# First chunk's attention: the products of probabilities and v of two heads, issued in alternation

## The chip, the cores and the metric

The kernel runs on one core of a Trainium2 chip. The metric is the device time of one execution in microseconds. Engines are named as in the profile: PE (TensorE; its weight loads are PEld), DVE (VectorE), ACT (ScalarE), POOL (GpSimd), SP (SyncE, which issues all DMAs).

## The reference

Attention with a decay for 4 batches of 8 heads (576 positions, head size 64), then a mixture of 4 experts over the 2304 tokens:

```python
scores = scale * np.matmul(q, k.transpose(0, 1, 3, 2))
log_f = np.log(np.clip(f, 0.0001, 1.0)); cum = np.cumsum(log_f, axis=-1)
scores = np.where(causal, -1e9, scores + cum[:, :, :, None] - cum[:, :, None, :])
attn = softmax(scores)                    # with 1e-09 added to the sum
x = np.matmul(attn, v)                    # as (2304, 512)
for e in range(4):                        # p = domain_probs, normalised
    out += p[:, e:e+1] * (np.maximum(x @ w1[e], 0) @ w2[e])
```

## The kernel before

Tokens are worked in nine chunks of 256. Chunk 0 is the first 256 positions of batch 0. The experts' products can only begin once the attention of chunk 0 is there, and from then on the attention of the other chunks runs between the experts' matmuls. So the program has a **startup**, the function `startup`, which does the attention of chunk 0 for 8 heads (4 pairs of heads, `Job`s with hh = 0 or 1), and a long rest.

The startup's instructions stand on each engine in the order in which they are written (`tc.manual_schedule()`). The rest, up to the last experts, is put in order by the tile framework's scheduler, which simulates the program as it is built: what changes in the startup moves it too.

A head of chunk 0 takes these steps, in fp32, each on the tiles that the profile names:

- scores: `qk_pe` (L760) writes two query tiles, 128x128 and 128x256, to PSUM (tile `s`). A matmul of the program in plain fp32 is two PE instructions of the profile (two passes).
- `qk_min` (L795, DVE) masks them, writes `p` and the row's bound `nm`; `qk_exp` (L810, ACT) takes the exponentials, 128 and 256 columns wide.
- `tr_pe` (L922, PE) turns `p` in three 128x128 transposes into PSUM tile `t`; `tr_copy` moves it to SBUF as `pt`, for hh = 0 on ACT (L930), for hh = 1 on DVE (L932).
- `av_pe` (L938, PE): two products with v, 256 and 128 columns (key tiles jt = 0 and 1), with 64 weight columns. The head hh = 0 writes partitions 0 to 63 of tile `o`, the head hh = 1 partitions 64 to 127 of the same tile: each head uses one half of the array's columns.
- once for a pair: `recip` (L830, L838 on DVE, L841 on POOL) and `spread` (L861, PE, tile `b`) for the sums, and `fin` (L977 on ACT, L978 on DVE), which scales `o` into `x`.

`startup` runs ten steps s. In a step, PE gets the scores of head s+1, then the spread of a finished pair (odd s from 3 on), the transposes of head s, and then the products of head s-1. In the second and third step four small filler matmuls on `mask` (`fill`, L251) stand ahead of the products. The products of head s-1 come one step after its transposes, so that the copy of `t` runs meanwhile. In the last pair the products of both heads follow each other.

The experts' matmuls of the rest are L1140, L1152 and L1195; the attention of later chunks has scores at L760 and products with v at L964 (`av_pair`, f16), where the matmuls of the two heads of a pair already alternate. Their probabilities reach them through DMA transposes (tile `pt`, L913).

Of the kernel before, what the change touches and what calls it, by code (L numbers as in the profile page):

```python
# [8 lines left out]
F32 = mybir.dt.float32  # L9
# [10 lines left out]
CH = 256  # L20
# [158 lines left out]
def fused(ctx: ExitStack, tc: tile.TileContext, qk, v, f, probs, w, out):  # L179
    nc = tc.nc  # L180
# [24 lines left out]
    ps_a = PS("ps_a", 4)  # L205
# [41 lines left out]
    def fill(ps, n):  # L247

        t = mask.bitcast(F16)
        for _ in range(n):  # L250
            nc.tensor.matmul(  # L251
                out=ps[:, 384:], lhsT=t[:, :128], rhs=t[:, :128], start=True, stop=True
            )
# [54 lines left out]
    def decay_parts():  # L308
        nc.scalar.activation(out=nc2[0], in_=ncum, func=AF.Copy)
        nc.vector.tensor_tensor(  # L310
            out=nc2[1], in0=ncum, in1=nc2[0].bitcast(F32), op=ALU.subtract
        )
        for n in range(2):
            nc.sync.dma_start(out=ncd[:, n], in_=nc2[n].bitcast(F32))

    def next_loads():
        for hh in range(2):
            jobs[NPR].load(hh)
            jobs[NPR].far(hh)
        v_load(1)  # L320
# [73 lines left out]
    def x_bound(b):  # L394

        def use(u, r):
            nc.vector.tensor_scalar(
                out=xun[:, b : b + 1], in0=u, scalar1=2.0**-2, scalar2=None, op0=ALU.mult
            )
            nc.vector.tensor_scalar(  # L400
                out=vsc[:, b : b + 1], in0=r, scalar1=2.0**14, scalar2=None, op0=ALU.mult
            )
            known.add(("x", b))

        def top():
            nc.vector.tensor_reduce(
                out=xsc[:, b : b + 1],
                in_=firsts[b].rearrange("p r t h d -> p (r t h d)"),
                op=ALU.max,
                axis=AX.X,  # L410
                apply_absolute_value=True,
            )

        across, exponent, finish = power(1, xsc[:, b : b + 1], f"x{b}", use)
        return top, across, exponent, finish
# [211 lines left out]
    class Job:  # L627
# [303 lines left out]
            else:  # L931
                nc.vector.tensor_copy(out=self.pt[hh], in_=self.tp[hh][:, :384])  # L932

        def av_pe(self, hh):
            if hh == 0:
                self.op[0] = ps_a.tile([128, 512], F32, tag="a", name=f"o{self.nm}")
            for jt in range(2):
                nc.tensor.matmul(  # L938
                    out=self.op[0][64 * hh : 64 * hh + 64, 128 * jt : CH],
                    lhsT=self.vr[:, jt, hh, :],  # L940
                    rhs=self.pt[hh][:, CH * jt : CH * jt + CH - 128 * jt],
                    start=(jt == 0),
                    stop=(jt == 1),
                )

        def av_pair(self):

# [124 lines left out]
    def w_load(n):  # L1072
        if n < 4 * WIDE and n not in wraw:
            if n >= 4 * WIDE - 2:
                wraw[n] = acc_p.tile([128, 1024], F32, tag="acc", name=f"wa{n}")
            elif n % 4 < 2:
                wraw[n] = w_p.tile([128, 1024], F32, tag="w", name=f"w{n}")
            else:
                wraw[n] = wr_p.tile([128, 1024], F32, tag=("wr", "wk")[n % 2], name=f"wr{n}", bufs=4)
            with tc.issue_after(gate[-1].ins) if len(gate) > 5 else nullcontext():  # L1080
                gate.append(nc.sync.dma_start(out=wraw[n], in_=w[unit(n)]))
        elif n in RAWS and n not in wraw:
            i = RAWS.index(n)
            wraw[n] = wr_p.tile([128, 1024], F32, tag=("wr", "wk")[i % 2], name=f"wr{n}", bufs=4)
            nc.sync.dma_start(out=wraw[n], in_=w[unit(n)])
# [853 lines left out]
    def startup():  # L1939

        J = lambda h: heads[h] if 0 <= h < FIRST else (None, None)
        decays()
        bound = x_bound(0)
        for h in range(2):
            heads[h][0].begin(h)
        heads[0][0].qk_pe(0, (0, 1))
        for t in range(2):
            heads[0][0].qk_min(0, t)
        for s in range(FIRST + 2):
            (m, mm), (j, hh), (i, ii), (k, kk) = J(s + 1), J(s), J(s - 1), J(s - 2)  # L1950
            if s == 2:
                bound[3]()
            if i:
                i.tr_copy(ii)
                if ii:
                    i.recip()
            if m:
                if s > 0:
                    m.begin(mm)
                m.qk_pe(mm, m.its)  # L1960
                for t in m.its:
                    m.qk_min(mm, t)
            if s == 1:
                bound[1]()
            if j:
                for t in j.its:
                    j.qk_exp(hh, t)
            if k and kk:
                k.spread()
            if j:  # L1970
                j.tr_pe(hh)
            if i:
                if s < 3:
                    fill(i.tp[ii], 4)
                i.av_pe(ii)
            if k and kk:
                k.fin()
            if s == 0:
                bound[0]()
            if s == 1:  # L1980
                bound[2]()
            for n in {0: (0, 1, 2, 3), 2: (4,), 3: (5,)}.get(s, ()):
                w_load(n)
            if s == 0:
                decay_parts()
            if s == 1:
                nc.sync.dma_start(out=pr_r, in_=probs)
            if s == 2:
                next_loads()
# [4 lines left out]
    with tc.manual_schedule():  # L1994
        startup()
# [161 lines left out]
```

## Time and profile before

| | us |
|---|---|
| median of 3 runs | 872.95 |
| runs | 872.12 to 874.1 |
| profiled execution | 873.64 |
| its span, first to last instruction | 871.8 |

The profiled execution is 0.69 above the median. Its span is 1.84 shorter than its own time. In a row of the timeline, the first two numbers are the start and the length in microseconds; consecutive instructions of one kind are merged (xcount), and a bracket gives the idle time of the engine before them and what ended it.

### The profile page before, as it was taken

How to read it: one execution, taken by the hardware profiler on the slowest of the kernel's cores; microseconds unless marked ns; L12 is line 12 of the kernel's file. 1: busy time of each engine (PE TensorE's matmuls, PEld its weight loads, DVE VectorE, ACT ScalarE, POOL GpSimd, SP SyncE). 2: the span in 40 equal slices, each digit the busy share in tenths (PEclk: the TensorE clock that was granted, in tenths of full speed). 3: DMA queues.
4: the chain of work that ended last, by engine and by line, in shares of the span. 5: the costliest groups of instructions: out<-in, count | busy, mean ns of one | idle time of the engine just before them, and what ended most of it. 6: DMA issues, size and time to landing. Idle time of an engine off the chain costs nothing.

```text
span 871.8 us, 16423 instructions
## 1 busy us (share of the span) xinstructions
PE 858.9 (99%) x5843; PEld 570.9 (65%) x5843; DVE 675.9 (78%) x1464; ACT 494.6 (57%) x1021; POOL 392.6 (45%) x439
## 2 busy tenths in 40 slices
PE   9999999999999999999999999999999999999998
PEld 5766666666666676766666666644466666666677
DVE  5866789868777888776768865546798988998897
ACT  5463645756555765656568653436655565655640
POOL 4253423543232422333332304907974898677530
PEclk9999999999999999999999999999999999999999
DMA  8999598799999899968979953433422343431103
GB/s 272 391 220 369 135 290 222 200 345 243 251 235 227 264 275 283 263 161 202 268 215 290 283 102 60 137 129 107 136 98 73 97 145 99 144 121 49 50 2 97
DMA packets 167679, 164.61 MB, mean 189 GB/s; under 512 B 104918, under 2 KB 129548, under 8 KB 167596
## 3 DMA queue, kind: packets, MB, share of 16 engines
q1 hardware_dynamic: 167596, 163.56, 67.4%
q8 instruction: 46, 0.75, 0.3%
q14 instruction: 37, 0.30, 0.1%
HBM read 117.75 MB, written 21.64 MB: 160 GB/s over the span
## 4 chain that ended last, share of the span: by engine, by line
PE 67%; DVE 12%; POOL 8%; DMA 5%; ACT 4%; issue 3%; SPq 1%; ACTq 0%; POOLq 0%; DVEq 0%
PE l L1195 18%; PE l L1152 15%; PE y L1527 10%; PE m L1527 8%; PE s L760 4%; PE o L964 3%; PE l L1140 3%; POOL wt L1344 3%; DMA raw<-in_qk 3%; DVE acc L1223 2%; PE s L783 2%; POOL bs L1416 2%; DVE w L1108 2%; DMA pt<-z 1%; DVE h L1590 1%
## 5 line engine op out<-in xcount | busy, mean ns | idle before, releaser
L1152 PE MATMUL l<-y,w 128*128 128x256 f16 x1728 | 211.5, 273 | 0.0
L1152 PEld LDWEIGHTS <-w 128*128 128x128 f16 x1728 | 163.8, 98 | 40.2 <-issue 7.6
L1195 PE MATMUL l<-w,gh 128*128 128x512 f16 (+1 forms) x600 | 184.4, 392 | 2.3 <-DVE acc L1223 1.7
L694 POOL CAST q<-raw 64x320 fp32r<-64x320 f32 (+1 forms) x56 | 25.2, 451 | 223.3 <-PE s L783 102.0
L1195 PE MATMUL l<-w,gl 128*128 128x512 f16 x284 | 107.2, 379 | 0.8 <-DVE gl L1169 0.8
L810 ACT ACTIVATE p<-p,nm 128x384 f32<-128x384 f32 (+3 forms) x96 | 62.0, 646 | 64.7 <-DVE nm L795 64.5
L1223 DVE SCALAR_TENSOR_TENSOR acc<-y,scg,acc 128x256 f32<-128x256 f32 (+1 forms) x204 | 93.8, 484 | 4.7 <-PE y L1527 4.6
L1527 PE MATMUL m<-rh,bs 128*128 128x512 f16 x256 | 86.4, 379 | 1.1 <-ACT r L1614 1.1
L1195 PEld LDWEIGHTS <-gh 128*128 128x128 f16 x568 | 51.1, 98 | 51.3 <-issue 10.7
L701 POOL TENSOR_TENSOR kl<-raw,hi 64x576 fp32r<-64x576 f32 (+1 forms) x56 | 66.5, 1188 | 38.7 <-ACT hi L692 35.1
L1527 PEld LDWEIGHTS <-h 128*128 128x128 f16 x672 | 65.7, 98 | 18.0 <-issue 0.6
L795 DVE CUSTOM_DVE_ANT_0 p<-s,mask 128x384 f32<-128x384 f32 (+3 forms) x96 | 54.3, 573 | 28.3 <-PE s L760 25.5
L898 DVE SCALAR_TENSOR_TENSOR z<-p,rs,z 128x512 f16<-128x512 f32 x96 | 61.0, 678 | 18.9 <-ACT z L897 18.9
L692 ACT ACTIVATE hi<-raw 128x896 fp32r<-128x896 f32 (+1 forms) x56 | 45.0, 807 | 37.9 <-DMA raw<-in_qk 16.5
L897 ACT ACTIVATE z<-p,rs 128x512 f16<-128x512 f32 x96 | 52.9, 613 | 22.5 <-issue 8.0
L1527 PE MATMUL m<-rh,bw 128*128 128x512 f16 x191 | 64.4, 379 | 0.1
L1169 DVE SCALAR_TENSOR_TENSOR gl<-l,gh 128x512 f16<-128x512 f32 x72 | 49.2, 683 | 17.5 <-ACT gh L1164 16.9
L1527 PEld LDWEIGHTS <-bs 128*128 128x128 f16 x384 | 37.5, 98 | 37.2 <-issue 1.6
L1527 PE MATMUL y<-bt,h 128*128 128x256 f16 x504 | 61.1, 273 | 0.3 <-DVE acc L1223 0.3
L1590 DVE SCALAR_TENSOR_TENSOR h<-s,h 128x512 f16<-128x512 f32 x56 | 58.2, 1050 | 2.0 <-ACT h L1584 1.7
L1416 POOL TENSOR_TENSOR bs<-wt,bs 128x512 f16<-128x512 f32 x32 | 42.5, 1338 | 35.9 <-ACT bs L1410 35.9
L1164 ACT ACTIVATE gh<-l 128x512 f16<-128x512 f32 (+1 forms) x80 | 46.9, 586 | 20.6 <-PE l L1152 17.8
(386 smaller groups left out, 1763.2 us busy)
## 6 DMA issues: line engine op xcount, KB each, us to landing
wr<-in_w SPq DMA_DIRECT2D x68, 512.0 KB
wd<-w SPq DMA_DIRECT2D x32, 512.0 KB
w<-wd SPq DMA_DIRECT2D x32, 512.0 KB
raw<-in_qk SPq DMA_DIRECT2D x32, 448.0 KB
wp<-in_w SPq DMA_DIRECT2D x36, 256.0 KB
bv<-wd SPq DMA_DIRECT2D x32, 256.0 KB
bw<-wd SPq DMA_DIRECT2D x32, 256.0 KB
raw<-in_qk SPq DMA_DIRECT2D x24, 256.0 KB
```

The costliest lines, as they stand in the source:

```text
L701: nc.gpsimd.tensor_tensor(out=kl[:64, :wk], in0=r[:64, ko : ko + wk], in1=hi[:64, ko : ko + wk].bitcast(F32), op=ALU.subtract,)
L795: nc.vector.tensor_tensor_reduce(out=pt[:, a:z], in0=ps, in1=mask2 if t == 4 and n else mask[:, m0 + a : m0 + z], scale=-0.125, scalar=BIG ...
L810: nc.scalar.activation(out=pt[:, :w_], in_=pt[:, :w_], func=AF.Exp, scale=-1.0, bias=self.nmax[hh][:, c : c + 1], accum_out=self.ssum[:, h ...
L897: nc.scalar.activation(out=o[:, 0], in_=x, func=AF.Copy, scale=sc)
L898: nc.vector.scalar_tensor_tensor(out=o[:, 1], in0=x, scalar=sc, in1=o[:, 0], op0=ALU.mult, op1=ALU.subtract)
L1152: nc.tensor.matmul(out=self.l1p[:, fi, :], lhsT=lhsT, rhs=rhs[:, k, :], start=(k == 0 and m == 0), stop=(k == 3 and m == 2),)
L1169: self.last = nc.vector.scalar_tensor_tensor(out=self.gl, in0=self.l1p, scalar=0.0, in1=self.gh, op0=ALU.max, op1=ALU.subtract,)
L1195: matmul(out=l2[tt], lhsT=lhsT, rhs=rhs, start=(opens and fi == 0 and m == 0), stop=(closes and fi == 1 and m == len(parts) - 1),)
L1223: i = nc.vector.scalar_tensor_tensor(out=acc[c][:, tt, d0:d1], in0=ps, scalar=sc, in1=acc[c][:, tt, d0:d1], op0=ALU.mult, op1=ALU.add,)
L1416: return nc.gpsimd.tensor_tensor(out=u[:, 1, a : a + 512], in0=got["f"][:, a : a + 512], in1=u[:, 0, a : a + 512], op=ALU.subtract,)
L1527: line.append(nc.tensor.matmul(**args))
L1590: return nc.vector.scalar_tensor_tensor(out=t[:, 1], in0=at_[key], scalar=0.0 if relu else 1.0, in1=t[:, 0], op0=op, op1=ALU.subtract,)
```

## The change

`av_pe` loses its argument: it is called once for a pair, where it was called for the second head, and issues the products of both heads with the heads alternating inside each key tile.

```diff
--- before.py
+++ after.py
@@ -931,17 +931,17 @@
             else:
                 nc.vector.tensor_copy(out=self.pt[hh], in_=self.tp[hh][:, :384])
 
-        def av_pe(self, hh):
-            if hh == 0:
-                self.op[0] = ps_a.tile([128, 512], F32, tag="a", name=f"o{self.nm}")
+        def av_pe(self):
+            self.op[0] = ps_a.tile([128, 512], F32, tag="a", name=f"o{self.nm}")
             for jt in range(2):
-                nc.tensor.matmul(
-                    out=self.op[0][64 * hh : 64 * hh + 64, 128 * jt : CH],
-                    lhsT=self.vr[:, jt, hh, :],
-                    rhs=self.pt[hh][:, CH * jt : CH * jt + CH - 128 * jt],
-                    start=(jt == 0),
-                    stop=(jt == 1),
-                )
+                for hh in range(2):
+                    nc.tensor.matmul(
+                        out=self.op[0][64 * hh : 64 * hh + 64, 128 * jt : CH],
+                        lhsT=self.vr[:, jt, hh, :],
+                        rhs=self.pt[hh][:, CH * jt : CH * jt + CH - 128 * jt],
+                        start=(jt == 0),
+                        stop=(jt == 1),
+                    )
 
         def av_pair(self):
 
@@ -1972,7 +1972,8 @@
             if i:
                 if s < 3:
                     fill(i.tp[ii], 4)
-                i.av_pe(ii)
+                if ii:
+                    i.av_pe()
             if k and kk:
                 k.fin()
             if s == 0:
```

On PE, in the startup, here at the pair 1 of batch 0 (`o0_1_0`; `s0_2_0_1` are the scores of pair 2, head 1; `t` are transposes). Before:

```order
L938 MATMUL o0_1_0_382<-pth_first_180,first3_189 64x256
L938 MATMUL o0_1_0_382<-pth_first_180,first3_189 64x128
L760 MATMUL s0_2_0_1_0_0_397<-first1_187 128x128
L760 MATMUL s0_2_0_1_0_0_397<-first1_187 128x256
L922 MATMUL t0_2_0_0_404<-ident_111,p0_2_0_0_0_363 128x128
L922 MATMUL t0_2_0_0_404<-ident_111,p0_2_0_0_1_364 128x128 x2
L938 MATMUL o0_1_0_382<-ptl_first_181,first3_189 64x256
L938 MATMUL o0_1_0_382<-ptl_first_181,first3_189 64x128
L760 MATMUL s0_3_0_0_0_0_416<-first2_188 128x128
L760 MATMUL s0_3_0_0_0_0_416<-first2_188 128x256
```

and now, from the same place on:

```order
L760 MATMUL s0_2_0_1_0_0_394<-first1_187 128x128
L760 MATMUL s0_2_0_1_0_0_394<-first1_187 128x256
L922 MATMUL t0_2_0_0_401<-ident_111,p0_2_0_0_0_363 128x128
L922 MATMUL t0_2_0_0_401<-ident_111,p0_2_0_0_1_364 128x128 x2
L938 MATMUL o0_1_0_405<-pth_first_180,first3_189 64x256
L938 MATMUL o0_1_0_405<-ptl_first_181,first3_189 64x256
L938 MATMUL o0_1_0_405<-pth_first_180,first3_189 64x128
L938 MATMUL o0_1_0_405<-ptl_first_181,first3_189 64x128
L760 MATMUL s0_3_0_0_0_0_416<-first2_188 128x128
L760 MATMUL s0_3_0_0_0_0_416<-first2_188 128x256
```

The two products of head 0 that stood behind the transposes `t0_1_0_1` are gone from there and now alternate with those of head 1, one pair of scores and one set of transposes later. The same happens at pairs 0 and 2; at pair 3, where the two heads' products already followed each other, only their order changes.

Behind the startup the scheduler's order differs on all engines up to about 190 us of the trace before, and is the same after that. One place of it, on DVE, at the attention of batch 2, pair 0 (`s2_0_0_0` and `s2_0_0_1` are the scores of its two heads, `nm` their bounds, `ss` the row sums, `wmax` a weight tile's maximum). Before:

```order
L795 ISA s2_0_0_0_0_0_1021,nm2_0_0_0_1005<-s2_0_0_0_0_0_1021,mask_112 128x256
L795 ISA nm2_0_0_0_1005 128x1
L795 ISA s2_0_0_1_0_0_1058,nm2_0_0_1_1044<-s2_0_0_1_0_0_1058,mask_112 128x256
L795 ISA nm2_0_0_1_1044 128x1
L1169 SCALAR_TENSOR_TENSOR gl4_4_0_0_1264<-l1_4_4_0_0_1207,gh4_4_0_0_1262 128x512
L422 TENSOR_REDUCE wmax_119<-wr26_932 128x2
L422 TENSOR_REDUCE wmax_119<-wr27_935 128x2
L851 TENSOR_SCALAR ss2_0_0_1006<-ss2_0_0_1006 128x2
L1223 SCALAR_TENSOR_TENSOR acc0_891<-l2_2_2_0_0_0_976,sc0_130,acc0_891 128x512
L851 TENSOR_SCALAR ss2_0_0_1006<-ss2_0_0_1006 128x2
```

and now:

```order
L795 ISA s2_0_0_1_0_0_1058,nm2_0_0_1_1044<-s2_0_0_1_0_0_1058,mask_112 128x128
L795 ISA nm2_0_0_1_1044 128x1
L795 ISA s2_0_0_0_0_0_1021,nm2_0_0_0_1005<-s2_0_0_0_0_0_1021,mask_112 128x256
L795 ISA nm2_0_0_0_1005 128x1
L795 ISA s2_0_0_1_0_0_1058,nm2_0_0_1_1044<-s2_0_0_1_0_0_1058,mask_112 128x256
L795 ISA nm2_0_0_1_1044 128x1
L851 TENSOR_SCALAR ss2_0_0_1006<-ss2_0_0_1006 128x2
L854 RECIPROCAL rs2_0_0_1007<-ss2_0_0_1006 128x2
```

The two maxima of weights that stood between the bounds and the sums are now ahead of the scores, and the reciprocal follows the sum. On PE the products `o2_0_0` come after fewer matmuls there: between the last scores of `s2_0_0_1` and the first product there were 58 of L1152 and 18 of L1195 (four of these in fp32), and now there are 24 and 24, all in f16; 12 products of another pair, 8 of scores and 2 small ones stand there in both.

## Rows read from the trace of the kernel before

**Rows 1.** The page: busy time, share of the span, instructions; granted clock by slice.

```profile
PE 858.9 (99%) x5843; PEld 570.9 (65%) x5843; DVE 675.9 (78%) x1464; ACT 494.6 (57%) x1021; POOL 392.6 (45%) x439
...
PEclk9999999999999999999999999999999999999999
```

**Rows 2.** Waits of PE from 27.8 to 205 us: total, times, longest.

```profile
PE l L1195 <- DVE acc L1223: 0.6, 1, 0.6
PE o L964 <- DMA pt<-z: 0.5, 1, 0.5
PE l L1195 <- DVE gl L1169: 0.3, 1, 0.3
```

**Rows 3.** Timeline of PE in the startup, first pair of heads.

```profile
12.80 0.86 PE L938 MATMUL o<-pth_first,first 128*64 128x256 f32 x4
...
13.82 0.35 PE L354 MATMUL topx<-ux,ones_r 1*128 1x1 f32 x2 [0.15 <-DVE ux L347]
...
15.58 0.87 PE L938 MATMUL o<-pth_first,first 128*64 128x256 f32 x4
```

**Rows 4.** Single lines of the source: shortest, median, longest ns of one instruction, first and last start.

```profile
L938 PE MATMUL o<-pth_first,first x4: 272/326/431, 12.8 to 13.4; 128*64 128x256 f32 x2, 128*64 128x128 f32 x2
...
L1140 PE MATMUL l<-x,w x18: 378/379/382, 27.8 to 39.4; 128*128 128x256 f32 x18
```

**Rows 5.** Timeline of PE, DVE and ACT in the startup, one cycle of two heads.

```profile
16.38 0.92 PE L760 MATMUL s<-first 128*128 128x128 f32 x4
...
17.34 0.29 DVE L795 CUSTOM_DVE_ANT_0 p<-s,mask 128x128 f32<-128x128 f32 x1 [1.24 <-PE s L760]
17.35 0.49 PE L922 MATMUL t<-ident,p 128*128 128x128 f32 x3
...
17.77 0.86 PE L938 MATMUL o<-pth_first,first 128*64 128x256 f32 x4
...
18.13 0.49 ACT L810 ACTIVATE p<-p,nm 128x256 f32<-128x256 f32 x1
...
18.57 0.92 PE L760 MATMUL s<-first 128*128 128x128 f32 x4
...
19.33 0.49 PE L922 MATMUL t<-ident,p 128*128 128x128 f32 x3
...
20.54 0.92 PE L760 MATMUL s<-first 128*128 128x128 f32 x4
```

**Rows 6.** Timeline of ACT and PE at the end of the startup.

```profile
24.79 0.50 ACT L810 ACTIVATE p<-p,nm 128x256 f32<-128x256 f32 x1
...
25.43 0.44 PE L922 MATMUL t<-ident,p 128*128 128x128 f32 x2 [0.16 <-ACT p L810]
...
25.80 1.69 PE L938 MATMUL o<-pth_first,first 128*64 128x256 f32 x8
...
27.54 0.44 PE L861 MATMUL b<-ident,x_first 128*128 128x128 f32 x2
...
27.81 1.03 PE L1140 MATMUL l<-x,w 128*128 128x256 f32 x4
```

**Rows 7.** Timeline in f16: products with v, two heads alternating, and a later run of L1152.

```profile
55.03 0.52 PEld L964 LDWEIGHTS <-v 128*64 128x64 f16 x11 [0.76 <-issue]
55.04 0.68 PE L964 MATMUL o<-pt,v 128*64 128x256 f16 x11
...
97.56 1.70 PE L1152 MATMUL l<-y,w 128*128 128x256 f16 x14
```

**Rows 8.** Timeline of batch 2, pair 0: scores, what follows, products with v.

```profile
90.67 0.28 PE L760 MATMUL s<-kl,q 66*128 66x256 f32 x1
...
94.31 0.63 ACT L692 ACTIVATE hi<-raw 128x512 fp32r<-128x512 f32 x1 [3.11 <-DMA raw<-in_qk]
...
96.76 2.34 DVE L422 TENSOR_REDUCE wmax<-wr 128x2 f32<-128x1024 f32 x2
...
107.06 0.30 PE L964 MATMUL o<-pt,v 128*64 128x256 f16 x1
```

## The prediction

> **What bounds the kernel now.** I read the page first, then the waits, then the timeline of the startup. PE is busy for 858.9 of 871.8 us and at its full granted clock in every slice [rows 1], so the kernel ends when PE has got through its work, and time is won only where PE's work shrinks or a wait of PE does. From the end of the startup (27.8 us) to 205 us PE waits for others for 1.4 us in three places [rows 2]. The reader is to see two things there: what the startup ends earlier is carried on by PE to the end, and behind it there is little waiting left to win. So the question is what the change takes from the startup, 5.5 to 27.8 us, and the startup is read cycle by cycle: two heads from one pair's scores to the next [rows 5].
>
> **Prices on PE.** A pass of 256 fp32 columns starts 0.216 us after the one before: four of L1140 take 1.03 us, of which the last runs 0.38, so (1.03 - 0.38) / 3 [rows 4, 6]. Three transposes of 128 columns take 0.49 us, the last 0.27, so 0.11 each [rows 5]. One head's products are four PE instructions, passes of 256, 256, 128 and 128 columns. Their starts spread over 0.86 - 0.27 = 0.59 us [rows 3, 4], and with the columns of the last that is 0.70: columns 2 x 0.216 + 2 x 0.11 = 0.65 and 0.05 more, lost at the first.
>
> A visit to these products costs more than its columns. The transposes that begin at 17.35 have fed their columns by 17.68, and the products begin at 17.77: 0.09 lost. The products are fed by 18.47, and the scores begin at 18.57: 0.10 lost. Those scores spread their starts over 0.92 - 0.38 = 0.54, where the passes of 128, 128 and 256 columns ahead of the last one need 0.11 + 0.11 + 0.22 = 0.43: 0.11 lost [rows 5]. With the 0.05 a visit costs 0.35 us beside its columns.
>
> **What the change does to PE's work.** There are seven visits before and four now: three fewer, 3 x 0.35 = 1.05 us less. The alternation matters too, as the two heads use different halves of the array's columns. In f16 such alternation is in the trace: 11 products, five of 256 columns and six of 128, are over 0.68 us after the first of them starts. A 256-column f16 matmul costs 0.11 us in a run, (1.70 - 0.27) / 13 at L1152, so one after the other these would need 5 x 0.11 + 6 x 0.055 = 0.88 for their columns alone [rows 7]. So the halves work side by side. In fp32 nothing like it is in the trace. The bounds are no overlap, 2 x 0.65 = 1.29 us of columns for a pair, and complete overlap, 0.65. I take a value between: a matmul of the program is two passes on the same half, so PE sees A A B B A A B B and, starting them in order, can lay the second pass of A beside the first of B but not the first of A. Laid out with the passes above: A at 0 and 0.215, B at 0.215 and 0.43, A at 0.43 and 0.54, B at 0.645 and 0.755, end at 0.86. A pair then costs 0.86, not 1.29: 0.43 less for each of four pairs, 1.72 us. PE's work falls by 1.05 + 1.72 = 2.77 us if halves overlap so.
>
> **How much of that reaches the end of the startup.** Not all, because another chain takes over. First pair: the visit at 12.80 is gone, but the next matmul, L354 at 13.82, already waits for DVE [rows 3], so the 0.7 us become a wait. The next visit still begins at 15.58 and holds both heads: 0.05 + 0.86 = 0.91 us instead of 0.70, so the scores at 16.38 come 0.21 later, at 16.59.
>
> Then two cycles of two heads, 20.54 - 16.38 = 4.16 us each. In one, the scores of the first head start at T. DVE takes them at T + 0.96 (17.34), the second exponential ends on ACT at T + 2.24 (18.13 + 0.49) [rows 5], and the second transpose of that head can start 0.14 later, as at the end of the startup, where it waits for exactly that (24.79 + 0.50, then 25.43) [rows 6]: T + 2.38. Before, PE came to these transposes at T + 2.95 (19.33), and nothing waited. Now PE reaches them after scores (0.76 with the 0.11), spread (0.22), three transposes (0.33) and scores without the loss (0.65), at T + 1.96, and the second one at T + 2.07. It waits 0.31 for the exponential. Then come two transposes (0.22), the entry (0.09), the products (0.91) and the exit (0.10): T + 3.70. A cycle is 0.46 shorter, not the 0.78 that PE's work falls by. Two cycles: 0.92 less, with the 0.21 of the first pair 0.71 less.
>
> Last pair: no gain. From the transposes at 25.43 the chain goes over DVE's copy and sums and POOL to the spread at 27.54 [rows 6], 2.1 us, and the products, done some 0.4 us sooner, are not its last link. So L1140 starts at 27.81 - 0.71 = 27.10.
>
> **Behind the startup.** The scheduler's new order has no price of its own in the columns. One visit to the f16 products fewer (of nine pairs that are split in two visits before, eight are now) saves about 0.3 us by the price of a visit above. One place looks tighter, batch 2, pair 0. Before, from the end of the scores (90.67 + 0.28) to the first product (107.06) were 16.1 us [rows 8]. In the new order PE has there 24 x 0.11 + 24 x 0.22 (512 columns, f16) + about 2 for the rest = 9.9 us. But two blocks of the old chain are gone from it: ACT stood behind a raw load until 94.31 (3.1 us), which the scores, now some 5 us later on PE, no longer meet, and the two maxima on DVE (2.3 us) now stand ahead [rows 8]. 16.1 - 3.1 - 2.3 = 10.7, so I expect a wait between 0 and 1 us and take 0.4. Weights are no new wait: PE waits for none of their loads [rows 2].
>
> **The sum.** 873.64 - 0.71 - 0.30 + 0.40 = 873.03 for an execution like the profiled one, which lies 0.69 above the median: 872.3 us. A measurement of this kernel can tell about 0.2% from no change, 1.75 us, so this is no change that can be told.
>
> **The rivals.**
> 1. The passes overlap completely: both heads in 0.65 + 0.05. The first pair then loses nothing, a cycle is 3.49, 0.67 less, two cycles 1.34. That is 0.63 more than in the forecast: 871.7. The Trainium skill says this (TensorE: Matmul & The Clock Gate, Part 3): matmuls on different tiles of the array start about 4 ns apart and a packed group takes one matmul's time and that much for each further tile. The f16 rows bear it out for single passes; for two passes on one half, starts in order speak against it. Chance 0.10.
> 2. fp32 halves don't overlap at all. A visit takes 1.34, the first pair loses 0.64, a cycle is 4.13, and the last scores still wait for ACT, so that the startup ends about 0.15 later: 873.2. The same part of the Trainium skill has a rule that speaks for it: a weight load overlaps with running matmuls only where their row groups differ, and here both heads use all rows. The f16 rows disagree: 11 weight loads run within the 11 products (0.52 of 0.68 us), on all 128 rows [rows 7]. Chance 0.16.
> 3. The waits of PE in the startup don't appear, because the chain over DVE and ACT is shorter than read, and all 2.77 us come through: 873.64 - 2.77 + 0.10 - 0.69 = 870.3. For it speaks that PE never waits in these cycles now; against it the wait of 0.16 at 25.43, where the chain is already bare [rows 6]. Chance 0.11.
> 4. Slower: at batch 2, pair 0, the chain to the probabilities keeps one of its blocks, or meets another load. PE then stands at `o2_0_0`: with one block of 3.1 us left 872.3 + 3.1 = 875.4, with both over 877. It decides the result from a wait of about 2.8 us on. For it: PE has only 9.9 us there, and DMA queues are busy. Against it: the order shows DVE's block moved. Chance 0.11.
> 5. The hole of about 1.1 us in front of L354 lets the granted clock fall to 1.2 GHz for some microseconds, though waits as long leave it at full speed elsewhere [rows 1]. If a cycle's PE work of some 3.4 us ran at half the clock, that costs 3.4 us at most, about half of it hidden: 874.0 to 875.7. Chance 0.03.
>
> **How the numbers follow.** The forecast has 0.49, its own range 871.2 to 873.5 (the place above at 0 to 1 us, other waits of the new order by about 1). Rivals 1 and 2 lie within 0.2% as well. Faster than 871.2: most of rival 3 (0.09), a third of rival 1 (0.03), 0.08 of the forecast: 0.20. Slower than 874.7: rival 4 (0.08), half of rival 5 (0.02), 0.03 from the tails of the others: 0.13. The rest, 0.67, is no change. The range reaches down past rival 3, 870.0, and up to 874.6, and leaves out rivals 4 and 5 and the tails.
>
> **What would show it right or wrong.** Of L938 four visits of eight PE instructions, each with starts spread over about 0.8 us (0.65 by rival 1, 1.2 by rival 2). A wait of PE for ACT's `p` of about 0.3 us at the transposes once a cycle, and one for DVE at L354 of about 1 us. The first L1140 near 27.1. At `o2_0_0` a wait under 1 us. The prediction is wrong if L1140 starts before 26 or after 28.2, or if waits of PE between 27 and 205 us differ from 1.4 by more than 1.5 us.

## The result: slower, by 0.7%

| | us |
|---|---|
| kernel before, median of 4 runs | 872.99 |
| changed kernel, median of 4 runs | 879.31 (878.71 to 881.03) |
| ratio | 1.007, 95% interval 1.0053 to 1.0087 |
| profiled execution of the changed kernel, and its span | 879.75, 878.0 |

The forecast was 872.3 in a range of 870.0 to 874.6, so it was wrong. In the profiles the startup did better than forecast and gave back 1.2 us, and the rest lost 7.4 us. The rows of the changed kernel that answer to [rows 1] (page: busy time, granted clock) show PE with less of the span and at its full clock:

```profile
PE 856.5 (98%) x5843; PEld 569.2 (65%) x5843; DVE 677.5 (77%) x1464; ACT 494.7 (56%) x1021; POOL 387.7 (44%) x439
...
PEclk9999999999999999999999999999999999999999
```

The waits of PE from 27.8 to 205 us, the answer to [rows 2] (total, times, longest):

```profile
PE topx L333 <- DVE y L993: 3.2, 1, 3.2
PE l L1195 <- DVE gl L1169: 2.2, 2, 1.9
PE o L964 <- DMA pt<-z: 1.6, 2, 0.8
PE l L1195 <- DVE acc L1219: 0.8, 1, 0.8
PE s L760 <- DVE z L898: 0.6, 1, 0.6
```

These are 8.4 us where [rows 2] have 1.4: seven microseconds more, nearly the whole of the 7.4. The startup, the answer to [rows 3, 5, 6] (timeline of PE: start, length, idle time before):

```profile
13.78 0.35 PE L354 MATMUL topx<-ux,ones_r 1*128 1x1 f32 x2 [0.95 <-DVE ux L347]
...
16.34 0.92 PE L760 MATMUL s<-first 128*128 128x128 f32 x4
...
18.30 0.27 PE L922 MATMUL t<-ident,p 128*128 128x128 f32 x1
18.74 0.44 PE L922 MATMUL t<-ident,p 128*128 128x128 f32 x2 [0.16 <-ACT p L810]
19.10 0.43 PE L938 MATMUL o<-pth_first,first 128*64 128x256 f32 x1
19.11 0.43 PE L938 MATMUL o<-ptl_first,first 128*64 128x256 f32 x1
19.37 0.38 PE L938 MATMUL o<-pth_first,first 128*64 128x256 f32 x1
19.38 0.38 PE L938 MATMUL o<-ptl_first,first 128*64 128x256 f32 x1
...
19.91 0.92 PE L760 MATMUL s<-first 128*128 128x128 f32 x4
...
26.56 1.68 PE L1140 MATMUL l<-x,w 128*128 128x256 f32 x7
```

The two heads' passes start 6 or 7 ns apart, in turns: both heads together take 0.81 us from the first product to the next scores (19.10 to 19.91), where one head took 0.80 [rows 5]. A cycle is 19.91 - 16.34 = 3.57 us instead of 4.16.

The startup's own beginning differs from profile to profile: the first filler (L251) started between 9.28 and 10.67 us. So I measure from that filler on. From it to the first L1140 the kernel before takes 18.02 us and the changed kernel 16.81: 1.21 us gained. From L1140 to the end the kernel before takes 844.0 us and the changed kernel 851.4.

### The profile page after: what moved, and what is told of

The parts are those of the page before. It is cut to its first block, busy times and chain, and to the rows that moved or that the text cites. A ratio compares the mean times of both kernels' runs of the same rounds, so it can differ in the third digit from the quotient of the medians.

```text
span 878.0 us, 16416 instructions
## 1 busy us (share of the span) xinstructions
PE 856.5 (98%) x5843; PEld 569.2 (65%) x5843; DVE 677.5 (77%) x1464; ACT 494.7 (56%) x1021; POOL 387.7 (44%) x439
## 4 chain that ended last, share of the span: by engine, by line
PE 68%; DVE 11%; POOL 9%; DMA 5%; ACT 4%; issue 3%; SPq 0%; POOLq 0%; ACTq 0%; DVEq 0%
PE l L1195 19%; PE l L1152 16%; PE y L1527 10%; PE m L1527 8%; PE s L760 4%; PE o L964 4%; DMA pt<-z 3%; PE l L1140 3%; POOL wt L1344 3%; PE s L783 2%; DVE acc L1223 2%; POOL bs L1416 2%; DVE w L1108 2%; POOL s L1650 1%; DMA raw<-in_qk 1%
## 5 line engine op out<-in xcount | busy, mean ns | idle before, releaser
L1152 PE MATMUL l<-y,w 128*128 128x256 f16 x1728 | 210.9, 273 | 0.0
L1152 PEld LDWEIGHTS <-w 128*128 128x128 f16 x1728 | 164.0, 98 | 39.8 <-issue 7.7
L1195 PE MATMUL l<-w,gh 128*128 128x512 f16 (+1 forms) x600 | 184.1, 392 | 2.6 <-DVE acc L1223 1.1
L1195 PE MATMUL l<-w,gl 128*128 128x512 f16 x284 | 107.1, 379 | 2.7 <-DVE gl L1169 2.7
L1195 PEld LDWEIGHTS <-gh 128*128 128x128 f16 x568 | 51.1, 98 | 51.4 <-issue 11.0
L1169 DVE SCALAR_TENSOR_TENSOR gl<-l,gh 128x512 f16<-128x512 f32 x72 | 49.2, 684 | 21.3 <-ACT gh L1164 20.9
L1164 ACT ACTIVATE gh<-l 128x512 f16<-128x512 f32 (+1 forms) x80 | 46.9, 586 | 27.5 <-PE l L1152 17.0
L692 ACT ACTIVATE hi<-raw 128x896 fp32r<-128x896 f32 (+1 forms) x56 | 44.9, 807 | 28.7 <-issue 14.2
```

Source lines behind the costliest of these rows:

```text
L1152: nc.tensor.matmul(out=self.l1p[:, fi, :], lhsT=lhsT, rhs=rhs[:, k, :], start=(k == 0 and m == 0), stop=(k == 3 and m == 2),)
L1169: self.last = nc.vector.scalar_tensor_tensor(out=self.gl, in0=self.l1p, scalar=0.0, in1=self.gh, op0=ALU.max, op1=ALU.subtract,)
L1195: matmul(out=l2[tt], lhsT=lhsT, rhs=rhs, start=(opens and fi == 0 and m == 0), stop=(closes and fi == 1 and m == len(parts) - 1),)
```

## Experiments: the order behind the startup

The scheduled part has the same instructions in both kernels; its order is drawn by a scheduler that reckons with the startup. To hold it still, a recorded order was given back as edges between neighbours on each engine, which set issue order and add no wait:

```diff
     flow.go()
-    late.close()
+    late.close(); pinned(tc, 240)
...
+def pinned(tc, first):
...
+        for x, y in zip(row, row[1:]):
+            tc.add_manual_dep(
+                y, x.name, mybir.DependencyInfo(mybir.DependencyClass.NoSync, mybir.DependencyReason.DATA)
+            )
```

`row` is one engine's instructions in the recorded order. The edges bring no instructions with them (the profile counts 16423 with the old order and 16416 with the new one, with edges and without), but the kernel before was not run with its own order given back, so a small price of theirs was not measured by itself. Two kernels cross the startup with the order.

**New startup, old order** (the table of the kernel before on all five engines):

> The changed startup, and behind it the scheduled part in exactly the order of the kernel before on all five engines (a recorded table, held by edges that set issue order only). Theory A, the loss lies in the order that the scheduler drew anew: the startup's gain stays (first-layer product L1140 at 26.56 instead of 27.81 us, -1.25) and nothing is lost behind it, 872.99 - 1.25 = 871.7 us. Theory B, the loss comes from the startup itself, because a stage that starts 1.25 us earlier runs ahead of its transfers or because the alternated products cost something later: 879.3 us as the changed kernel has it, with PE's waits between 27 and 205 us near 8.6 us.

**Old startup, new order** (the table of the changed kernel):

> The startup of the kernel before, and behind it the scheduled part in exactly the order of the changed kernel. Theory A (the new order costs): 872.99 + (879.31 - 872.99 + 1.25) = 880.6 us, with the 3.2 us wait before L333 of topx3. Theory B (the startup itself costs): 873.0 us. If both have a share, this run and the one with the old order add up to the change: the differences to 872.99 sum to 6.3 us.

Measured: 0.9996 (0.9988 to 1.0005) with the new startup and the old order, 1.0068 (1.0053 to 1.0084) with the old startup and the new order. The loss is in the order: with the old order the new startup loses nothing, and with the new order the old startup loses about as much as the changed kernel. In the second kernel PE's waits are nearly those of the changed kernel, though its startup is the old one:

```profile
PE topx L333 <- DVE y L993: 2.8, 1, 2.8
PE l L1195 <- DVE gl L1169: 2.1, 2, 1.7
PE o L964 <- DMA pt<-z: 1.4, 3, 0.6
PE s L760 <- DVE z L898: 1.0, 1, 1.0
```

**Does it take this change to draw such an order?** Two kernels changed only trifles of the startup and left the order to the scheduler. In the first, from the kernel before, one of twelve warm-up matmuls (L245) is left out:

```diff
-AWAKE = 12
+AWAKE = 11
```

> The kernel before with 11 instead of 12 warm-up matmuls (L245) ahead of the first load; its startup has nothing else changed, and the order of the scheduled part is drawn anew by the scheduler (239 rows of PE differ from before, 491 from the changed kernel). If any shift of the startup in the scheduler's own reckoning draws an order whose time is a matter of luck: a difference to before of over 0.2%, with PE waits between 27 and 205 us that are not those of before (1.4 us). If the loss needs this change's early lead: 873.0 us within 0.2%.

In the second, from the changed kernel, there are two filler matmuls more:

```diff
-                    fill(i.tp[ii], 4)
+                    fill(i.tp[ii], 5)
```

> The changed kernel with five instead of four filler matmuls (L251) at each of the two places where they stand ahead of the products, some 0.1 us on PE each; the scheduler draws a third order (254 rows of PE differ from before, 478 from the changed kernel). If the order decides: not 879.3 but a time of its own, nearer to 873 us since its order is nearer to that of before. If the change itself decides: 879.3 us.

Measured: the kernel before with one warm-up matmul less 1.0039 (1.0026 to 1.0052), the changed kernel with two fillers more 1.0039 (1.0027 to 1.0051). Neither has the time of its parent. The first is the telling one: its startup takes the same 18.01 us on the chip as that of the kernel before (18.02), and it loses 3.4 us behind L1140. The longest of PE's waits in it, from 27.8 to 205 us:

```profile
PE l L1195 <- DVE gl L1169: 2.1, 2, 1.8
PE s L760 <- DVE z L898: 0.9, 1, 0.9
```

So both trifles that were tried redrew the order, and all three redrawn orders here were slower than the one of the kernel before.

## Experiments: what in the new order costs

**One wait taken away.** The largest wait is at the transpose L333 into `topx3`. It takes the PSUM buffer of `o2_0_0`, the products of batch 2, pair 0, and their readers (y, L992 and L993) stand on ACT and DVE behind the splitting of weights (L1107, L1108):

```profile
107.52 4.40 ACT L1107 ACTIVATE w<-wr,wsc 128x512 f16<-128x512 f32 x7 [0.90 <-DVE wsc L469]
110.48 2.88 DVE L1108 SCALAR_TENSOR_TENSOR w<-wr,wsc,w 128x512 f16<-128x512 f32 x4
115.03 0.41 DVE L993 SCALAR_TENSOR_TENSOR y<-o,y 128x256 f16<-128x256 f32 x1
115.59 0.27 PE L333 MATMUL topx<-ident,xsc 128*1 128x128 f32 x1 [3.21 <-DVE y L993]
```

In the changed kernel's own order one matmul was moved (PE's order, shortened):

```diff
 L1152 l1_4_4_1_1
-L333 topx3
 L1195 l2_4_4_1_0 ... (12)
 L1152 l1_5_5_0_0 ... (8)
+L333 topx3
```

> The changed kernel with its own order on all engines, except that one matmul, the transpose L333 into topx3, stands behind the 8th of the twelve L1152 products that come 12 matmuls after it (l1_5_5_0_0, first weight tile), about 3.5 us later on PE. If the wait of 3.2 us for DVE's y (L993), which holds the PSUM buffer that topx3 takes, is lost time of its own: 879.3 - 3.2 = 876.1 us, with no wait before L333. If it only stands in for a wait that comes next (gh and gl of the same group, acc): 879 us, with the 3.2 us found again before 130 us.

Measured: 1.0069 (1.0052 to 1.0085), nothing gained. The 3.2 us before L333 are gone, and PE waits for ACT's gh and longer for `pt` instead:

```profile
PE o L964 <- DMA pt<-z: 2.9, 4, 1.0
PE l L1195 <- ACT gh L1164: 2.9, 1, 2.9
```

**The short operations ahead of the splits.** Next, ACT's and DVE's order was changed so that y, gh and gl (gh, L1164 on ACT, and gl, L1169 on DVE, are an expert's hidden values and the remainder of their f16 rounding) no longer stand behind the run of splits (DVE shown, ACT alike; at a second place `gl6_6_1_1` ahead of the last four pieces):

```diff
 L1108 w20, w21 (4 pieces)
+L993 y2 <- o2_0_0
+L1169 gl4_4_1_0
 L1108 w22, w23 (4 pieces)
-L993 y2 <- o2_0_0
-L1169 gl4_4_1_0
```

> The changed kernel with its own order, except at the two places where ACT and DVE split eight weight pieces in a row (107.5 to 115 us and 168 to 176 us): ACT's y (L992 of o2_0_0) and gh (L1164 of gh4_4_1_0) and DVE's y (L993) and gl (L1169) now stand ahead of the pieces of the second weight pair (w22, w23), and at the second place DVE's gl6_6_1_1 stands ahead of the last four of its eight pieces. PE's order is untouched. If the waits of 3.2 us (L333 for y) and 1.85 us (L1195 for gl) are there because these four short operations stand behind a run of splits: 879.3 - 5.05 = 874.3 us, and both waits under 0.6 us. If ACT and DVE are simply short of time there, so that the wait only moves to the next operation, as it did when topx3 alone was moved: 877 to 880 us.

Measured: 1.0073 (1.0058 to 1.0088). Both waits are gone as ordered, and others have come:

```profile
PE s L760 <- DVE ss L851: 3.2, 1, 3.2
PE o L964 <- DMA pt<-z: 2.0, 4, 1.1
PE topv L333 <- DVE y L993: 1.4, 1, 1.4
```

So neither wait was time to be won by itself: each time others came in its place. The reading that fits both runs is that PE runs out of ready work there, and whichever instruction stands next shows the wait. What is late is the attention as a whole. One landmark tells it in each run: the conversion of the first raw tile of batch 2, pair 1 (`hi2_1_0_0`, ACT L692). Before and after:

```profile
90.57 0.62 ACT L692 ACTIVATE hi<-raw 128x512 fp32r<-128x512 f32 x1
```

```profile
96.27 0.63 ACT L692 ACTIVATE hi<-raw 128x512 fp32r<-128x512 f32 x1
```

**Why it is late.** In the stretch 50 to 75 us the transfers ran dry in the new order, and behind it they were crowded (busy times by engine, granted clock, busy share of the DMA engines, GB/s; before, then after):

```profile
50.00:75.00 25.00, 25.00 (x113) 15.90 (x112) 18.95 (x59) 16.28 (x41) 11.98 (x14) 1.00 0.87 291
75.00:100.00 25.00, 24.39 (x137) 16.23 (x136) 14.82 (x46) 11.55 (x34) 7.57 (x13) 1.00 1.00 265
```

```profile
50.00:75.00 25.00, 25.00 (x117) 16.67 (x116) 16.94 (x50) 15.00 (x37) 9.68 (x14) 1.00 0.74 233
75.00:100.00 25.00, 24.35 (x128) 15.47 (x127) 18.27 (x55) 11.59 (x35) 7.54 (x13) 1.00 1.01 308
```

PE shows none of this: it is as busy in both. SP issues every transfer, in order. In its timeline (before, then after; the row of DVE's z is set ahead) the transposing transfers `pt` (L913), which wait for DVE's z, stand ahead of the weight loads (L1081):

```profile
55.20 0.48 DVE L898 SCALAR_TENSOR_TENSOR z<-s,rs,z 128x256 f16<-128x256 f32 x1 [0.84 <-ACT z L897]
55.71 3.83 SPq L913 DMA_TRANSPOSE pt<-z  x3
...
60.23 0.41 SPq L1081 DMA_DIRECT2D w<-in_w  x1
```

```profile
57.64 0.48 DVE L898 SCALAR_TENSOR_TENSOR z<-s,rs,z 128x256 f16<-128x256 f32 x1 [1.30 <-ACT z L897]
58.15 1.23 SPq L913 DMA_TRANSPOSE pt<-z  x1
...
60.84 3.79 SPq L913 DMA_TRANSPOSE pt<-z  x3
...
65.64 0.80 SPq L1081 DMA_DIRECT2D w<-in_w  x2
```

In both the first transpose is issued 0.03 us after z ends (55.68 and 58.12). The transposes come 2.4 us later, and the first load of L1081 5.4 us later; part of these 5.4 is SP's order itself, in which a fourth transpose and two other loads now stand ahead of it. Going back from there, SP's order differs in little: two swaps of neighbours near 23 and 36 us, and then one load (`raw1_2_0_0`, L650) that stands two transfers later. The orders of PE, DVE and ACT differ from about 30 us on, and these differences were not tested one by one. Two kinds of runs tested SP.

**SP alone exchanged.** All other engines keep their order; only the table of SP is that of the other kernel:

> The changed kernel with its own order on PE, DVE, ACT and POOL; only SP, the queue that issues every transfer, has the order of the kernel before. In the runs with a redrawn order the transfers run dry between 50 and 75 us (busy share 0.67 to 0.74 instead of 0.87) because loads stand on SP behind transposing transfers (L913) that wait for DVE's z, and the raw tiles of batch 2 come 3 to 6 us later. If SP's order is the cause: share back to 0.85 or more, 872 to 874 us. If SP only waits because the other engines make z later: share under 0.78 and 878 to 880 us.

> The changed startup with the order of the kernel before on PE, DVE, ACT and POOL, and SP alone in the changed kernel's order. If SP's order carries the loss: busy share of the transfers between 50 and 75 us near 0.72, and 877 to 880 us. If it carries none: 873.7 us as in the run with the old order on all engines.

Measured: 1.0352 (1.0334 to 1.0369) and 1.0175 (1.0156 to 1.0194). Both expectations fell: each mixture is far worse than either pure order. With SP's old order in the new kernel the busy share of the transfers between 50 and 75 us is 0.58, lower still. Not all of this loss is waiting: in these two profiles PE's mean granted clock is 0.988 and 0.992, which over spans of 902.5 and 887.1 us withholds about 11 and 7 us of full clock (some of it while PE waits anyway). The reading is that SP's order fits the order of the engines that make z and free the buffers, and cannot be judged apart from them. These two runs don't tell which engine's order is at fault; exchanging PE's or DVE's order alone was not tried.

**One load moved.** In the changed kernel the load goes forward to its old place, and in the kernel before it goes back to the new one, with all else in the own order of each:

```diff
+L650 raw1_2_0_0
 L913 pt1_0_0_1 (second)
 L1085 wr18
-L650 raw1_2_0_0
```

> The changed kernel with its own order on every engine, except one transfer: on SP the load of raw1_2_0_0 (L650) stands two transfers earlier, ahead of the second transposing transfer of pt1_0_0_1 and of the load wr18, where the kernel before has it (47.3 us instead of 49.5 us). If that one late load starts the chain (raw tile 2.2 us later, scores and z later, SP's transposing transfers at 58.2 instead of 55.7 us, the loads behind them at 65.6 instead of 60.2 us), the chain ends 2 us earlier and the time is 875 to 877 us. If it is one of many: 879 us.

> The kernel before with its own order on every engine, except that on SP the load of raw1_2_0_0 (L650) stands two transfers later, behind the second transposing transfer of pt1_0_0_1 and the load wr18, where the changed kernel has it: the mirror of the run in which that load was moved ahead. If this one load starts a chain by itself (load 2.2 us later, transposing transfers and the loads behind them later, the raw tiles of batch 2 later), the conversion of the first raw tile of batch 2, pair 1 (ACT L692, 62.8 us after L1140 starts) comes 1 us or more later and the time is 0.6 to 2 us above that of before. If the order of before absorbs it: no change within 0.2%, and that conversion within 0.5 us of 62.8.

Measured: moved forward 1.0058 (1.0039 to 1.0077), against 1.007 of the changed kernel: in the right direction, but the intervals overlap, so a gain is not shown. Moved back in the kernel before: 1.0025 (1.0014 to 1.0036), slower by 2.2 us through the place of one 256 KB load (the edges can't be all of it: with them, the two kernels with the new startup and the old order were at 0.9996 and 0.9989). SP's timeline of this run shows the end of the chain as read: z ends at 58.80 instead of 55.68 us, the transposes come at 58.84 instead of 55.71, the weight load at 63.35 instead of 60.23:

```profile
58.32 0.48 DVE L898 SCALAR_TENSOR_TENSOR z<-s,rs,z 128x256 f16<-128x256 f32 x1 [0.39 <-ACT z L897]
58.84 3.83 SPq L913 DMA_TRANSPOSE pt<-z  x3
62.76 0.54 SPq L650 DMA_DIRECT2D raw<-in_qk  x1
63.35 0.41 SPq L1081 DMA_DIRECT2D w<-in_w  x1
```

All profiles but those of the two mixtures side by side, ordered by the landmark. "Startup" is from the first filler to L1140, "rest" from there to the end, "waits" are all idle times of PE in the first 180 us of the rest, "landmark" is the start of `hi2_1_0_0` after L1140; all from single instructions of the profiles, in us:

| kernel | startup | rest | waits | landmark | ratio |
|---|---|---|---|---|---|
| before | 18.02 | 844.0 | 1.6 | 62.8 | 1 |
| new start, old order | 16.80 | 845.4 | 2.3 | 62.8 | 0.9996 |
| same, acc before wmax (below) | 16.81 | 843.8 | 1.6 | 62.8 | 1.0000 |
| same, heads one after the other (below) | 16.82 | 845.0 | 2.1 | 63.9 | 0.9989 |
| before, one load later | 18.01 | 845.4 | 2.6 | 64.5 | 1.0025 |
| before, one warm-up less | 18.01 | 847.4 | 4.2 | 66.5 | 1.0039 |
| changed, one load earlier | 16.81 | 848.9 | 5.4 | 68.6 | 1.0058 |
| changed, two fillers more | 16.87 | 851.2 | 6.8 | 69.0 | 1.0039 |
| changed | 16.81 | 851.4 | 8.7 | 69.7 | 1.0070 |
| changed, short operations first | 16.82 | 852.5 | 7.6 | 69.7 | 1.0073 |
| old start, new order | 18.02 | 850.9 | 7.2 | 70.1 | 1.0068 |
| changed, topx3 later | 16.81 | 854.0 | 9.4 | 72.2 | 1.0069 |

In these twelve the profiled rest grows by about 1 us for each microsecond that the landmark is late (844.0 at 62.8, 854.0 at 72.2). The timed ratios follow less evenly, and the two mixtures above (rest 860.2 at 67.6, 875.0 at 75.0) lie far off the line. One reason is that a profile is one execution and not always a middle one: that of "before, one load later" was the shortest of nine, that of "two fillers more" the second longest of ten. Another is the granted clock: in five of the twelve (one load earlier, two fillers more, short operations first, old start with the new order, topx3 later) it fell to half for some microseconds behind a wait, and PE lost up to 1.7 us by it; in the other seven it stayed at 1.00 in these 180 us. With the waits and this loss the rest of each of the twelve comes out within 1 us. So the landmark is a correlation over profiles, and lateness is shown as a cause for one load only. Which other places of the new order carry the remaining 5 us stays open.

## Experiments: what the startup's gain is worth

**One visit, but the heads one after the other** (A A B B; old order behind the startup):

```diff
-            for jt in range(2):
-                for hh in range(2):
+            for hh in range(2):
+                for jt in range(2):
```

> One visit for each pair as in the change, but the products stand A A B B, head after head, and the scheduled part has the order of the kernel before. If the merging of visits alone carries the startup's gain, L1140 starts at 26.6 us and the time is 871.7 us. If the alternation carries its share, a visit of a pair takes about 1.29 us instead of 0.87 (rows 5 and 7 of before: 4 x 0.216 + 4 x 0.11 for four products), the two middle cycles give back only the merged entries and exits, and L1140 starts between 26.9 and 27.5 us: 872.1 to 872.7 us.

Measured: 0.9989 (0.9977 to 1.0001), and a startup of 16.82 us, as with the alternation. The alternation, which gives the change its name, is worth nothing by itself; calling once for a pair does it all. The timeline shows why: although head 0's two matmuls stand first in the program, both heads' passes start side by side, 13 ns apart (what brings them side by side, no run here tells):

```profile
18.89 0.43 PE L938 MATMUL o<-pth_first,first 128*64 128x256 f32 x1
18.90 0.43 PE L938 MATMUL o<-ptl_first,first 128*64 128x256 f32 x1
19.15 0.38 PE L938 MATMUL o<-pth_first,first 128*64 128x256 f32 x1
19.17 0.38 PE L938 MATMUL o<-ptl_first,first 128*64 128x256 f32 x1
...
19.69 0.92 PE L760 MATMUL s<-first 128*128 128x128 f32 x4
```

**Where the 1.21 us go.** With the old order kept, the gain should have arrived whole, a ratio of 0.9986, and the two runs showed 0.4 and 0.9 us of it; the interval of the second (from 0.9977) holds the whole gain, that of the first (from 0.9988) just misses it. In both profiles PE loses part of its lead at one place, where [rows 2] have 0.6 us (here with the new start and the old order):

```profile
100.07 0.59 PE L1195 MATMUL l<-w,gh 128*128 128x512 f16 x2 [1.34 <-DVE acc L1223]
```

DVE is late there because ACT, in order, waits at 94.3 us for a raw tile [rows 8], which lands at about the same time however early the startup ends (94.50 us in this run), and two weight maxima of 2.34 us stand ahead of acc. One more run put them behind it:

```diff
+L1223 acc0 (2)
 L422 wmax (2)
-L1223 acc0 (2)
```

> The changed startup with the order of the kernel before, except that two reductions on DVE (wmax of two raw weight tiles, L422, 2.34 us) stand behind the two accumulations acc (L1223) instead of ahead of them, near 97 us. In the run with the old order PE lost at that place what the startup had gained: it waited 1.34 us for acc instead of 0.61 us, since DVE stands behind scores whose raw tile lands at 94.3 us whenever the startup ends. If that is the whole of the missing gain, PE no longer waits there and the time is 872.99 - 1.21 - 0.61 = 871.2 us. If the reductions' delay of 1.4 us or a later place takes it back: 873 us or more.

Measured: 1.0000 (0.9989 to 1.001). The wait is gone, and the profiled rest is 1.7 us shorter than with the old order alone, yet the timed runs show no gain. The profiles mislead here: the one with the old order alone lies 0.75 us above its kernel's median, this one 0.95 below its own, which together is the whole of the 1.7. So it isn't shown that this place costs the timed runs anything; where the gain ends up in them is open, and a price of the edges of under a microsecond is not excluded. No version here beats the kernel before by more than its interval.

## Why the prediction was wrong, by its steps

- **What bounds the kernel.** That PE's work and waits make the time was right: the waits of PE are 7.0 of the 7.4 us lost. "What the startup ends earlier is carried on by PE to the end" is not borne out: with the old order 0.4 and 0.9 of 1.21 us were seen, and in the profiles the lead shrinks at a place that a transfer paces.
- **Price of a visit, first pair.** L354 waits 0.95 us for DVE, as forecast (about 1). The visit of a pair was forecast at 0.86 and its edge of 0.05, by passes in the order A A B B; it was 0.65 and the edge, complete overlap. Rival 1 had this right. The Trainium skill's rule behind it (TensorE: Matmul & The Clock Gate, Part 3) has matmuls on different tiles of the array about 4 ns apart; here the starts lie 6 to 13 ns apart. The first pair lost 0.00 instead of 0.21.
- **The cycles.** PE reaches the transposes at T + 1.96 and passes the second one at T + 2.40 (16.34, 18.30, 18.74), where 1.96 and 2.38 were forecast. The cycle is 3.57 instead of 3.70: the overlap saves 0.21, and 0.08 of that went, most of it between the second transpose and the products (0.36 us, forecast at 0.31). The last pair gained nothing, as forecast. The term of the startup, -0.71, measured -1.21.
- **Behind the startup: the step that failed.** "The scheduler's new order has no price of its own in the columns", and +0.40 - 0.30 us for all that lies behind the startup. It measured +7.4, of which 7.0 are waits of PE (8.4 us instead of 1.4, beyond the 1.5 that the prediction named as its own sign of being wrong). No run shows the 0.30 by itself. I looked at one place of the new order, from PE's side, and at loads only by whether PE waits for them. The order of SP's queue I did not compare, and the transfers run dry from 50 to 75 us (busy share 0.74 instead of 0.87) while PE looks as busy as before. That the order costs this is shown by the crossed runs; how it does is shown for one load (2.2 us in the kernel before) and open for the rest.
- **Rivals 2 and 3** fell: a pair's products and their exit take 0.81 us where rival 2 had 1.34 for the products alone, and the waits that rival 3 left out are there (0.95 us at L354, 0.16 at the transposes of each cycle).
- **Rival 4** had the place (batch 2, pair 0), the sign and a price (875.4 to over 877), with a chance of 0.11. Its mechanism was half right: PE stands near `o2_0_0`, but at the matmul that takes its PSUM buffer, and that wait is a symptom, as two runs showed. A redrawn order deserved a much larger chance and range: the three kernels here with one were 0.4 to 0.7% slower.
- **Rival 5**, a clock hole in the startup, did not occur: the granted clock is 1.00 through the startup's products.

## What to carry to other kernels

When a scheduler orders the program, a small edit is two edits: its own, and a new draw of everything that the scheduler orders after it. Hold the order still (record it, give it back as issue-order edges) before judging the edit, and compare the order of the queue that issues transfers too: a load that stands two places later behind a waiting transfer cost 2.2 us here. A wait that is removed and comes back at the next instruction suggests that the engine has run out of ready work; look then for what is late upstream. And where an effect is near a microsecond, see where the profiled execution lies among the timed ones before reading a difference of two profiles.

## What was not expected of the hardware

- Products on the two column halves of the array run side by side in fp32 too, and even when the program has all of one half ahead of the other (A A B B); the weight loads of both heads lie inside. Two heads cost what one costs (0.81 us to the next scores against 0.80).
- A wait of PE of about 3 us can be followed by half the clock, or not. With the old startup and the new order PE stood 2.76 us before L333 at 116.81 us, and behind it the granted clock was 0.81, 0.50 and 0.84 in three stretches of 2 us, some 1.7 us of full clock withheld; in the changed kernel the wait of 3.21 us at the same instruction left it at 1.00. Such a stretch needn't show in the time: of the changed kernel's four timed executions two had a mean granted clock of 0.998, and they were the two shortest (878.71 and 878.86 us). The rows of the old startup with the new order:

```profile
116.00:118.00 2.00, 1.19 (x5) 0.60 (x6) 2.00 (x5) 2.00 (x8) 1.87 (x3) 0.81 0.87 324
118.00:120.00 2.00, 2.00 (x7) 0.62 (x6) 2.00 (x5) 0.74 (x3) 0.56 (x1) 0.50 1.02 418
120.00:122.00 2.00, 2.00 (x13) 1.23 (x12) 2.00 (x5) 0.00 (x0) 0.00 (x0) 0.84 1.06 430
```
